# Chunked attention and a squared-ReLU feed-forward on one core: other engines for three squares of the last block, one values step a slot later, and V loads behind transposes in two blocks

## The chip, the cores and the metric

The kernel runs on one core of a Trainium2 chip. The metric is device time in microseconds (us). Five engines with queues of their own matter here: TensorE (PE, with its weight loads listed as PEld), VectorE (DVE), ScalarE (ACT), GpSimd (POOL) and SyncE (SP), which issues nearly all DMAs. Each engine takes its instructions in the order in which the program lists them; an instruction that waits holds back everything behind it on the same engine.

## The reference

For 8 batches and 8 heads, sequences of 576 tokens with 64 values per head are cut into chunks of 64. Attention stays within a chunk. The result, seen as 4608 tokens by 512, goes through a two-layer network with a squared ReLU.

```python
scores = scale * np.matmul(q_c, k_c.transpose(0, 1, 2, 4, 3))     # per chunk of 64
attn = np.exp(scores - max);  attn = attn / (attn.sum(-1) + 1e-09)
out = np.matmul(attn, v_c)
x = out.transpose(0, 2, 1, 3).reshape(B * S, H * D)               # 4608 x 512
h = np.maximum(x @ w_in, 0.0)                                     # 4608 x 2048
return h * h @ w_out                                              # 4608 x 512
```

## The kernel before, in words

The 4608 tokens are 18 groups of 256 tokens (four chunks each); two groups make a block of 512, so there are blocks 0 to 8. Groups 14 and 15 (block 7) collect the ninth chunk of each batch; every other group is "whole", four neighbouring chunks of one batch.

While TensorE runs the feed-forward of block j, the attention of block j+1 (`nxt`) is put between its matmuls, and inputs of block j+2 (`far`) are loaded. The order is written out by hand. A block is a row of **slots**: each `yield` of `ffn_in`/`ffn_in_unit` and then of `ffn_out` ends one. After a slot, one DMA of the list `loads` is issued if the slot's number stands in `go_slots`, and then the steps that `at(slot, step, group)` planned there. For blocks from 3 on, `loads` holds six q and k loads and then nine V loads (first the even heads and odd heads of one group, then of the other; lines 148 and 152). The steps are:

- `C` (`CQ`, `CK`): cast q and k to bf16, on ScalarE for late groups; `TD`: SP's DMA transpose of them (L352);
- `SC`: the 64 score matmuls of a group (L375) and the exponential `e` on ScalarE (L386);
- `AV`: the values product of a group (L403), in two halves t = 0 and 1, each followed on VectorE by a reciprocal `rec` (L410) and a multiplication into `x` (L411);
- `XT`: SP's DMA transpose of `x` into `xT` (L424), which the next block's feed-forward reads.

Scores and values share a pool of two accumulator tiles, `ps_att`. SC of two groups fills both; each half of AV takes one, so half t = 1 of the first group needs the second group's `e` to have been read out, and the halves of the second group's AV need the first group's `x` multiplications done.

Blocks 4 to 8 (`UNITS`) use `ffn_in_unit`. Of the 16 tiles of the hidden layer (`ft`, 128 wide), twelve are done plainly: four matmuls (L608) into an accumulator, a ReLU on ScalarE into a tile `rl` (L572), and a square into `gT`. The square goes to VectorE, GpSimd (both L621, which is the line of the helper `add`) or ScalarE (L575), by a table: `UNIT_SQUARES` for blocks 4 to 7 and `LAST_SQUARES` for block 8, "P" for GpSimd, "A" for ScalarE, VectorE if the tile isn't named. The other four tiles, ft 4 to 7, are computed by seven products instead of eight (L495), one per "u" in `UNIT_ORDER`, in two accumulators `n` and `m` that are held through all seven. I number these steps u1 to u7:

- u1: n, copied to `n1` (ACT, L518). u2: m, and VectorE makes `w = m + n1`.
- u3: n again, copied to `n2` (ACT, L526). u4: m; VectorE makes `c21 = w - m`, GpSimd makes `c12 = w - n2`.
- u5: n; VectorE makes `s = n - n2`. u6: m; VectorE makes `c22 = m + s`, the last reader of m.
- u7: n; ScalarE makes the ReLU of it (L547), GpSimd squares that.

The squared ReLUs of c21, c12 and c22 are three VectorE instructions of another kind, SCALAR_TENSOR_TENSOR (L512), put behind slots 10, 11 and 14. The slots of such a block are: 0 to 2 for ft 8, 9, 10; then u1, ft 11, u2, ft 12, u3, ft 13 (slot 8), u4, ft 14 (slot 10), u5 (11), ft 15 (12), u6 (13), ft 0 (14), u7 (15), ft 1, 2, 3 (16 to 18); then 14 slots of `ffn_out`. The accumulators of the plain tiles come from a pool of four, of which n and m hold two; ft 2's is the one that c22 sets free.

`ffn_out` multiplies the four quarters of `gT` (ft 0 to 7 and 8 to 15, first and second 256 tokens) with the second weight by the same kind of seven products, 16 matmuls each (L661): the first reads ft 8 to 15, the second ft 0 to 7, the others differences that VectorE makes (L621, `w_st<-gT`), beginning with one that needs all of `gT`.

Of the kernel before, what the change touches and what calls it, by code (L numbers as in the profile page):

```python
# [17 lines left out]
def kernel(  # L18
# [31 lines left out]
    def is_whole(g):  # L50
        return chunks[g][0][0] == chunks[g][3][0]
# [104 lines left out]
    def go(pieces):  # L156
        for f in pieces:
            f()
# [279 lines left out]
    SC, AV, XT = scores, values, transpose_x  # L438
# [111 lines left out]

    UNIT_ORDER = (8, 9, 10, "u", 11, "u", 12, "u", 13, "u", 14, "u", 15, "u", 0, "u", 1, 2, 3)
    UNIT_SQUARES = {10: "P", 13: "P", 14: "P", 15: "P", 0: "P", 1: "A", 2: "A", 3: "A"}
    LAST_SQUARES = {10: "P", 13: "P", 14: "P", 12: "A", 1: "A", 2: "A"}
    UNIT_LATER = (10, 11, 14)

    def ffn_in_unit(j):
# [7 lines left out]
        for i, ft in enumerate(UNIT_ORDER):  # L564
            if ft == "u":
                next(products)
            else:
# [4 lines left out]
                nc.scalar.activation(out=rl, in_=h, func=AF.Relu)  # L572
                by = (UNIT_SQUARES if j + 1 < len(blocks) else LAST_SQUARES).get(ft)
                if by == "A":
# [8 lines left out]
    def ffn_in(j, parts, begun={}):  # L583
        if j not in gTs:
            gTs[j] = ffn_pool.tile([128, n_ft, BT], BF16, name="gT")
        gT, xT = gTs[j], xTs[j]
        for u, (c, n, ft) in enumerate((c, n, ft) for c, n, fts in parts for ft in fts):
            h = begun.get(ft)
            if h is None:
                h = ps_ffn.tile([128, 512], FP32, name="ps_ffn")  # L590
            for dt in range(n_dt // 2 if ft in begun else 0, n_dt):
                ffn_in_step(h, xT, c, n, ft, dt)
            if j < 3:
                if n == 512 or u % 2 == 0:
                    rl_tile = ffn_pool.tile([128, 512], FP32, name="rl", bufs=5).bitcast(BF16)
                rl = rl_tile[:, u % 2 * 512:] if n < 512 else rl_tile
            else:
                rl = rl_tile_fp32()
            nc.scalar.activation(out=rl[:, 0:n], in_=h[:, 0:n], func=AF.Relu)  # L599
            if (n == 512 and ft in SQUARES_ON_ACT) or (n < 512 and ft in (12, 3)):  # L600
                nc.scalar.activation(out=gT[:, ft, c:c + n], in_=rl[:, 0:n], func=AF.Square)
            else:
                nc.vector.tensor_tensor(  # L603
                    out=gT[:, ft, c:c + n], in0=rl[:, 0:n], in1=rl[:, 0:n], op=ALU.mult)
            yield
# [17 lines left out]
    def sum_quarters(out, in0, in1, op=ALU.add, half=slice(None)):  # L623
        return lambda _: add(nc.vector, out[:, half], in0[:, half], in1[:, half], op)
# [124 lines left out]
    def ffn_out_by_ft(j):  # L749

        gT = gTs.pop(j)
        n_tt = len(blocks[j]) * GT // 128
        o_ps = [ps_ffn.tile([128, d_model], FP32, name="ps_ffn") for _ in range(n_tt)]

        def mm(tt, ft):
            nc.tensor.matmul(  # L756
                out=o_ps[tt],
                lhsT=gT[:, ft, tt * 128:(tt + 1) * 128],
                rhs=w_out_bf[:, ft, :],
                start=(ft == 0), stop=(ft == n_ft - 1))  # L760


        for ft in range(n_ft - 4):
            for tt in range(n_tt - 1 if ft == 0 else n_tt):
                mm(tt, ft)
                if ft == 1 and tt == n_tt - 2:
                    mm(n_tt - 1, 0)
            yield
        for tt in range(n_tt):
            for ft in range(n_ft - 4, n_ft):  # L770
                mm(tt, ft)
            o_sb = ffn_pool.tile([128, d_model], FP32, name="o_sb", bufs=4)
            nc.scalar.copy(out=o_sb, in_=o_ps[tt])
            b, s0 = chunks[blocks[j][tt // 2]][0]
            t0 = b * S + s0 + tt % 2 * 128
            nc.gpsimd.dma_start(out=out[t0:t0 + 128, :], in_=o_sb)
            yield

    def pieces(grps):
        for g in grps:  # L780
            yield from qk_pieces(g)
        for g in grps:
            yield from v_pieces(g)
# [3 lines left out]
    A, V = nc.scalar.copy, nc.vector.tensor_copy  # L787
# [53 lines left out]
    for j, grps in enumerate(blocks):  # L841
        nxt = blocks[j + 1] if j + 1 < len(blocks) else []
        far = blocks[j + 2] if j + 2 < len(blocks) else []
        plan = {}

        def at(slot, f, g):
            plan.setdefault(slot, []).append((f, g))

        if j == 0:
            loads, go_slots = pieces(far), range(17)  # L850
            at(28, sum_quarters(b11_p_b21, b11, b21), None)
            for slot, f in ((24, TA), (27, SC), (29, AV), (31, XT)):
                at(slot, f, nxt[0])
            at(31, TQ, nxt[1])
            at(31, TK, nxt[1])
            at(31, sum_quarters(b11_m_b22, b11, b22, ALU.subtract), None)
            phases = [first_ffn_in, ffn_out_by_ft(0)]
        elif j == 1:
            loads, go_slots = itertools.chain(*map(qk_pieces, far)), range(26, 48)
            for slot, f in ((4, SC), (8, AV), (12, XT)):  # L860
                at(slot, f, grps[1])
            for i, g in enumerate(nxt):
                for slot, f in ((16 + 4 * i, C), (21 + 4 * i, TD), (36 + i, SC), (38 + 2 * i, AV),
                                (41 + 2 * i, XT)):
                    at(slot, f, g)
            for i, g in enumerate(far):
                at(36 + 4 * i, C, g)
                at(42 + 3 * i, TD, g)
            at(2, sum_quarters(b11_p_b12, b11, b12), None)
            at(12, sum_quarters(b12_p_b22, b12, b22), None)  # L870
            at(20, sum_quarters(b21_p_b22, b21, b22), None)
            phases = [ffn_in(1, [(0, 256, FT_ORDER), (256, 256, FT_ORDER)]), ffn_out(1)]
        else:
            loads, go_slots = pieces(far), range(32)
            slots = {SC: (4, 4), AV: (7, 11), XT: (10, 14), C: (18, 22), TD: (20, 24)}
            if j == 3:
                slots.update({SC: (8, 8), AV: (10, 14), XT: (13, 17)})
                go_slots = [*range(6), *range(13, 32)]
            if not is_whole(nxt[0] if nxt else 0):
                slots.update({SC: (6, 8), AV: (10, 14), XT: (12, 16)})  # L880
            if j == 2:
                loads = itertools.chain(*map(v_pieces, nxt), loads)
                slots = {SC: (8, 10), AV: (12, 15), XT: (15, 18), C: (20, 23), TD: (22, 25)}
                go_slots = [*range(16), *range(25, 36)]
            late_by = 0
            if j in UNITS:
                late_by = 3
                go_slots = [*range(6), *range(13, 17), *range(23, 35)] if j == 4 else range(35)
                slots.update({SC: (4, 4), AV: (8, 13), XT: (12, 17)})
                if not is_whole(nxt[0] if nxt else 0):  # L890
                    slots.update({SC: (8, 8), AV: (10, 14), XT: (14, 18)})
            if j == 3:
                at(2, w_differences, None)
            for f in (SC, AV, XT):
                for i, g in enumerate(nxt):
                    at(slots[f][i], f, g)
            if j > 2 and far and is_whole(far[0]):
                for slot, f, i in ((16, CQ, 0), (18, CK, 0), (18, TD, 0), (18, CQ, 1),
                                   (19, CK, 1), (19, TD, 1)):
                    at(slot + late_by, f, far[i])  # L900
            else:
                for f in (C, TD):
                    for i, g in enumerate(far):
                        at(slots[f][i] + late_by, f, g)
            phases = [ffn_in_unit(j) if j in UNITS else ffn_in(j, [(0, BT, FT_ORDER)]),
                      ffn_out(j)]
        slot = 0
        for phase in phases:
            for _ in phase:
                if slot in go_slots:  # L910
                    for f in loads:
                        f()
                        break
                for f, g in plan.get(slot, []):
                    f(g)
                while late and slot >= LATE_STORES[j]:
                    late.pop(0)()
                slot += 1
        assert all(x < slot for x in plan), (j, slot, sorted(plan))
        go(loads)  # L920
        while late:
            late.pop(0)()
# [30 lines left out]
```

## Time and profile before

| what | us |
|---|---|
| median of the 3 runs (lowest, highest) | 284.1 (282.72, 285.33) |
| the profiled execution's own time | 280.75 |
| its span | 279.0 |
| TensorE busy | 268.4 |
| VectorE, ScalarE, GpSimd busy | 199.2, 156.9, 82.3 |

All times inside a block are taken from the profiled execution, counted from the start of its span. Block 3 runs there from about 110 to 138 us, block 4 to 165, block 5 to 193, block 6 to 221, block 7 to 248 and block 8 to the end. A matmul's recorded end is some time after the next one may begin (they are pipelined), so I read pitches, from start to start: four matmuls of a plain tile 0.86 us, a product of the unit 0.44 us.

### The profile page before, as it was taken

To read this page: it belongs to the slowest core of one execution; us is meant where nothing else is said; L and a number is where in the kernel's file an instruction comes from. 1 tells how busy PE (TensorE), PEld (TensorE's weight loads), DVE (VectorE), ACT (ScalarE), POOL (GpSimd) and SP (SyncE) were. 2 spreads that over 40 slices of the span, in tenths; PEclk is the share of its full clock that TensorE was granted. 3 is DMA by queue.
4 is the path that set the end of the run, shared out by engine and by line. 5 is a ranking of instruction groups with operands and counts; after the bars stand their busy time and mean duration, and the time that the engine had idled before them with its cause. 6 is when DMAs were issued, how large, how long until landed. Compare 5 with 4: busy or idle time off the path is not lost.

```text
span 279.0 us, 7336 instructions
## 1 busy us (share of the span) xinstructions
PE 268.4 (96%) x3020; PEld 182.9 (66%) x3023; DVE 199.2 (71%) x311; ACT 156.9 (56%) x264; POOL 82.3 (29%) x100
## 2 busy tenths in 40 slices
PE   7889999999999999999999999999999999999895
PEld 4543444888774487448765876587558765876484
DVE  0546514998947695579869776987697769876793
ACT  1537605895358853877186927682858276227610
POOL 2037734161169000000029002800470038004412
PEclk9999999999999999999999999999999999999999
DMA  7999999999999999999999999859898942150003
GB/s 236 219 317 361 365 339 237 324 228 191 239 238 194 241 222 203 262 231 195 233 286 239 178 248 253 189 123 221 234 232 180 191 154 53 25 135 18 0 0 150
DMA packets 144384, 57.09 MB, mean 205 GB/s; under 512 B 110624, under 2 KB 141600, under 8 KB 144352
## 3 DMA queue, kind: packets, MB, share of 16 engines
q1 hardware_dynamic: 143296, 53.62, 83.5%
q0 software_dynamic: 912, 2.88, 2.8%
q8 instruction: 23, 0.38, 0.6%
q10 hardware_dynamic: 144, 0.13, 0.1%
q14 instruction: 9, 0.07, 0.1%
HBM read 36.70 MB, written 9.44 MB: 165 GB/s over the span
## 4 chain that ended last, share of the span: by engine, by line
PE 78%; DVE 5%; SPq 4%; DMA 4%; issue 3%; ACT 3%; POOL 2%; POOLq 0%
PE ps_ffn L661 32%; PE ps_ffn L608 32%; PE ps_ffn L756 5%; PE ps_ffn L495 5%; SPq L237 3%; DVE gT L603 2%; DMA qkT<-qkb 2%; PE ps_att L403 2%; DMA w_st<-in_moe_w_in_dram 2%; DVE x L411 1%; PE ps_att L375 1%; ACT rl L599 1%; ACT e L386 1%; POOL gT L621 1%; SPq L228 1%
## 5 line engine op out<-in xcount | busy, mean ns | idle before, releaser
L608 PE MATMUL ps_ffn<-xT,w_in_bf 128*128 128x512 bf16 (+1 forms) x560 | 116.5, 355 | 2.1 <-DVE rl L621 1.4
L608 PEld LDWEIGHTS <-w_in_bf 128*128 128x128 bf16 x560 | 53.5, 98 | 45.0 <-POOL w_in_bf L166 2.0
L621 POOL TENSOR_TENSOR gT<-rl 128x512 bf16<-128x512 f32 x28 | 32.7, 1180 | 131.5 <-ACT rl L572 130.8
L661 PEld LDWEIGHTS <-w_st 128*128 128x128 bf16 x640 | 62.0, 98 | 7.9 <-DVE w_st L621 0.6
L621 DVE TENSOR_TENSOR w_st<-gT 128x2048 bf16<-128x2048 bf16 x40 | 47.4, 1220 | 6.3 <-ACT gT L575 6.2
L603 DVE TENSOR_TENSOR gT<-rl 128x256 bf16<-128x256 bf16 (+2 forms) x67 | 36.0, 573 | 21.6 <-ACT rl L599 20.7
L572 ACT ACTIVATE rl<-ps_ffn 128x512 f32<-128x512 f32 x60 | 35.8, 596 | 22.0 <-PE ps_ffn L608 22.0
L599 ACT ACTIVATE rl<-ps_ffn 128x512 bf16<-128x512 f32 (+2 forms) x80 | 39.0, 511 | 12.4 <-PE ps_ffn L608 11.4
L661 PE MATMUL ps_ffn<-w_out_bf,w_st 128*128 128x256 bf16 x384 | 45.1, 273 | 0.1
L661 PE MATMUL ps_ffn<-w_sum,w_st 128*128 128x256 bf16 x256 | 29.6, 273 | 0.0
L621 DVE TENSOR_TENSOR gT<-rl 128x512 bf16<-128x512 f32 x22 | 15.4, 702 | 17.8 <-ACT rl L572 17.5
L661 PEld LDWEIGHTS <-gT 128*128 128x128 bf16 x256 | 24.6, 98 | 4.9 <-ACT gT L575 0.7
L746 ACT COPY o_sb<-ps_ffn 128x512 f32<-128x512 f32 (+1 forms) x8 | 4.5, 560 | 38.9 <-PE ps_ffn L661 38.9
L411 DVE TENSOR_TENSOR x<-ps_att,rec 128x512 bf16<-128x512 f32 x32 | 22.1, 692 | 1.1
L386 ACT ACTIVATE e<-ps_att 128x1024 bf16<-128x1024 f32 x16 | 15.8, 1022 | 5.1 <-PE ps_att L375 5.1
L512 DVE SCALAR_TENSOR_TENSOR gT<-rl 128x512 bf16<-128x512 f32 x15 | 15.8, 1052 | 0.8 <-POOL rl L621 0.6
L661 PE MATMUL ps_ffn<-w_out_bf,gT 128*128 128x256 bf16 x128 | 15.6, 273 | 0.0
L661 PE MATMUL ps_ffn<-w_sum,gT 128*128 128x256 bf16 x128 | 15.3, 273 | 0.0
L756 PE MATMUL ps_ffn<-w_out_bf,gT 128*128 128x512 bf16 x61 | 14.2, 379 | 0.3 <-issue 0.2
L166 POOL CAST w_in_bf<-w_st 128x1024 bf16<-128x1024 f32 (+1 forms) x9 | 8.6, 959 | 18.8 <-DMA w_st<-in_moe_w_in_dram 18.8
L495 PEld LDWEIGHTS <-w_dif 128*128 128x128 bf16 x100 | 9.3, 98 | 5.3
L341 ACT CAST qkb<-k_sb 128x1024 bf16<-128x1024 f32 x10 | 10.5, 1046 | 1.2 <-DMA k_sb<-in_k_dram 1.2
(81 smaller groups left out, 270.7 us busy)
## 6 DMA issues: line engine op xcount, KB each, us to landing
q_sb<-in_q_dram SPq DMA_DIRECT2D x16, 512.0 KB, 5.8
k_sb<-in_k_dram SPq DMA_DIRECT2D x24, 256.0 KB, 5.9
out_dram<-o_sb SPq DMA_DIRECT2D x20, 256.0 KB, 3.1
w_st<-in_moe_w_in_dram SPq DMA_DIRECT2D x8, 512.0 KB, 7.4
w_st<-in_moe_w_out_dram SPq DMA_DIRECT2D x8, 512.0 KB, 6.1
ve_sb<-in_v_dram SPq DMA_DIRECT2D x28, 128.0 KB, 3.8
vo_sb<-in_v_dram SPq DMA_DIRECT2D x21, 128.0 KB, 3.3
out_dram<-o_sb POOLq DMA_DIRECT2D x9, 256.0 KB, 5.8
```

Source lines behind the costliest of these rows:

```text
L341: copy(out=state["qkb", g][:, 1], in_=qk[g][1].rearrange("p t h d -> p (t h d)"))
L386: nc.scalar.activation(out=e_out, in_=s_in, func=AF.Exp, scale=scale)
L411: nc.vector.tensor_tensor(out=x[:, t].rearrange("p h a d -> p a h d"), in0=o[:, :, :, 0:D], in1=rec.to_broadcast([128, 2, n_hp, D]), op=AL ...
L495: nc.tensor.matmul(out=out[:, 256 * f:256 * f + 256], lhsT=a[:, d, 128 * f:128 * f + 128], rhs=b[:, :, d, :], start=(first and f == 0 and ...
L512: later.append(lambda: nc.vector.scalar_tensor_tensor(out=place_of(i, jj), in0=both(x), scalar=0.0, in1=both(x), op0=ALU.max, op1=ALU.mult))
L572: nc.scalar.activation(out=rl, in_=h, func=AF.Relu)
L599: nc.scalar.activation(out=rl[:, 0:n], in_=h[:, 0:n], func=AF.Relu)
L603: nc.vector.tensor_tensor(out=gT[:, ft, c:c + n], in0=rl[:, 0:n], in1=rl[:, 0:n], op=ALU.mult)
L608: nc.tensor.matmul(out=h[:, 0:n], lhsT=w_in_bf[:, dt, ft * 128:(ft + 1) * 128], rhs=xT[:, c // 128:(c + n) // 128, dt, :], start=(dt == 0) ...
L621: engine.tensor_tensor(out=out, in0=in0, in1=in1, op=op)
L661: nc.tensor.matmul(out=outs[t], lhsT=a[:, i, t * 128:(t + 1) * 128], rhs=b[:, i, :], start=(first and i == 0 and (last or t == 0)), stop=( ...
L756: nc.tensor.matmul(out=o_ps[tt], lhsT=gT[:, ft, tt * 128:(tt + 1) * 128], rhs=w_out_bf[:, ft, :], start=(ft == 0), stop=(ft == n_ft - 1))
```

## The change

Three things change. In block 8, the square of ft 12 goes from ScalarE to VectorE, that of ft 13 from GpSimd to ScalarE, and that of ft 15 from VectorE to GpSimd. In block 6 (the unit block ahead of the groups that are not whole), AV of its two groups moves from slots 10 and 14 to 11 and 15. And `go_slots` leaves gaps: in block 3 slots 18 and 19 carry no load any more, so that five of the nine V loads come behind SP's transposes of x and of q, k; in block 6 the same list that block 4 already had is used, with four V loads in slots 13 to 16 and five from slot 23 on.

```diff
-    LAST_SQUARES = {10: "P", 13: "P", 14: "P", 12: "A", 1: "A", 2: "A"}
+    LAST_SQUARES = {10: "P", 14: "P", 15: "P", 13: "A", 1: "A", 2: "A"}
...
             if j == 3:
                 slots.update({SC: (8, 8), AV: (10, 14), XT: (13, 17)})
-                go_slots = [*range(6), *range(13, 32)]
+                go_slots = [*range(6), *range(13, 17), *range(20, 32)]
...
             if j in UNITS:
                 late_by = 3
-                go_slots = [*range(6), *range(13, 17), *range(23, 35)] if j == 4 else range(35)
+                go_slots = range(35)
+                if far and is_whole(far[0]):
+                    go_slots = [*range(6), *range(13, 17), *range(23, 35)]
                 slots.update({SC: (4, 4), AV: (8, 13), XT: (12, 17)})
                 if not is_whole(nxt[0] if nxt else 0):
-                    slots.update({SC: (8, 8), AV: (10, 14), XT: (14, 18)})
+                    slots.update({SC: (8, 8), AV: (11, 15), XT: (14, 18)})
```

No instruction is added or taken away; on every engine the same kinds and sizes run as before.

## The prediction

> **What bounds the kernel now.** I read the first part of the page, then TensorE's waits, then the stretches of `ffn_in` of three unit blocks, and last the timeline where TensorE stands still. The page:
>
> ```profile
> span 279.0 us, 7336 instructions
> PE 268.4 (96%) x3020; PEld 182.9 (66%) x3023; DVE 199.2 (71%) x311; ACT 156.9 (56%) x264; POOL 82.3 (29%) x100
> ```
>
> TensorE sets the pace: 10.6 us of the span are left, most of them in the start. What an edit can win is what TensorE still waits for in blocks 6 and 8. The stretches (columns after the length: busy us and instructions of PE, PEld, DVE, ACT, POOL, then the granted clock):
>
> ```profile
> 165.40:180.56 15.16, 15.16 (x206) 8.53 (x205) 11.30 (x20) 10.68 (x18) 8.20 (x7) 1.00 0.91 228
> 192.86:208.61 15.75, 15.54 (x207) 8.72 (x205) 11.72 (x20) 10.84 (x18) 8.38 (x7) 1.00 0.97 244
> 248.38:263.32 14.94, 13.57 (x79) 7.46 (x77) 10.08 (x13) 10.06 (x18) 6.10 (x5) 1.00 0.18 43
> ```
>
> Blocks 5, 6 and 8, each at clock 1.00. Block 6 takes 0.59 us more than block 5 for the same work. Block 8 has no attention to do and still takes 14.94, with 1.37 idle. TensorE's waits name both:
>
> ```profile
> PE ps_ffn L608 <- DVE rl L621: 1.4, 1, 1.4
> PE ps_att L403 <- ACT e L386: 0.2, 1, 0.2
> ```
>
> **Block 8.** Its timeline (start, length, engine, line):
>
> ```profile
> 254.24 0.63 ACT L575 ACTIVATE gT<-rl 128x512 bf16<-128x512 f32 x1
> 254.77 0.57 ACT L526 COPY n<-ps_ffn 128x512 f32<-128x512 f32 x1
> 255.92 1.04 POOL L621 TENSOR_TENSOR gT<-rl 128x512 bf16<-128x512 f32 x1 [3.14 <-ACT rl L572]
> 256.92 1.72 POOL L621 TENSOR_TENSOR rl<-nm,n 128x512 f32<-128x512 f32 x1
> ...
> 258.67 1.51 DVE L512 SCALAR_TENSOR_TENSOR gT<-rl 128x512 bf16<-128x512 f32 x1 [0.56 <-POOL rl L621]
> 260.10 0.68 DVE L621 TENSOR_TENSOR gT<-rl 128x512 bf16<-128x512 f32 x1
> 260.70 0.68 DVE L621 TENSOR_TENSOR rl<-ps_ffn,n 128x512 f32<-128x512 f32 x1
> 261.44 1.89 PE L608 MATMUL ps_ffn<-xT,w_in_bf 128*128 128x512 bf16 x8 [1.37 <-DVE rl L621]
> ```
>
> The reader sees a chain: the square of ft 12 on ScalarE holds up the copy n2; GpSimd's c12 waits behind the square of ft 13 and ends at 258.64; VectorE's squared ReLU of c12 waits for it; behind that stand the square of ft 15 and c22, which ends at 261.38; then ft 2 gets its accumulator. ft 1 began at 259.04, so by the pitch of 0.86 ft 2 could have begun at 259.90: the stall is 1.54 us (the 1.37 counts from the modelled end of ft 1).
>
> After the change, with the same durations: n2 follows the ReLU of ft 12 (254.11 to 254.70). c12 stands next behind the square of ft 10, which is long done: 254.75 to 256.05. VectorE: square of ft 12 254.24 to 254.93, c21 255.34 to 256.03, its squared ReLU to 256.75, s to 257.4. The squared ReLU of c12 meets GpSimd's square of ft 14 (256.85 to 257.89). In this trace such an instruction ends 0.55 us after the GpSimd operation that was running (258.67 beside one that ends at 259.63, done at 260.18; the 256.07 one in block 8 likewise), so 258.44. c22 then runs 258.37 to 259.05. That is 0.85 before ft 2 wants its accumulator: the stall goes, 1.54 us. The square of ft 13 on ScalarE (255.53 to 256.16) ends before ft 14's ReLU at 256.20. That of ft 15 on GpSimd ends by 259.5; its reader, the first output product, starts at 261.63.
>
> What is late next: ScalarE's squares of ft 1 and 2 and ReLU of ft 3 run back to back. Before they ended at 264.24, now ReLU of ft 1 260.10, square, ReLU of ft 2, square, ReLU of ft 3, at 0.63 each, end near 263.2; VectorE's square of ft 3 follows, 263.25 to 263.94. The second output product needs it with its fourth matmul, at 261.63 + 1.75 + 0.33 = 263.7. So 0.25 to 0.3 come back as a new wait, and the differences for the third product are as tight. I take **1.25 us gained**; bounds 1.54 and nothing.
>
> A rule speaks against this part. The row: GpSimd's operation at 260.34 took 1.34 instead of 1.04 us beside VectorE's square of 260.10. The Trainium skill, "SBUF — State Buffer", section "Who interferes with whom", says that a VectorE instruction with two inputs in SBUF and a GpSimd one that reads SBUF shut each other out. By it the square of ft 12, new on VectorE, delays c12 by up to 0.2; the sum stays, since c12 isn't needed before 257.4.
>
> **Block 6, values a slot later.** Half t = 1 of the first AV waited for the second `e` until 201.83; whole AV took 0.80 instead of 0.39. One product later it would start at 201.77, t = 1 at 201.94: no wait. Without a new wait, ft 1 of this block would start at 205.25 instead of 205.86, a gain of 0.61. But VectorE's order turns too: s and the squared ReLU of c12 now stand ahead of the first group's `x`. Before:
>
> ```profile
> 201.29 1.59 DVE L512 SCALAR_TENSOR_TENSOR gT<-rl 128x512 bf16<-128x512 f32 x1
> 202.81 0.19 DVE L410 RECIPROCAL rec<-ps_att 128x8 f32<-128x8 f32 x1
> 203.03 0.69 DVE L411 TENSOR_TENSOR x<-ps_att,rec 128x512 bf16<-128x512 f32 x1
> ```
>
> After it: s 202.81 to 203.49; the squared ReLU of c12 is issued at 203.41, while GpSimd squares ft 14 (until 203.78), and ends at 204.33; rec 204.26, x of t = 0 204.48 to 205.17, x of t = 1 205.32 to 206.01. The second AV, at slot 15, would like to start at 204.86, but its halves need those tiles: t = 0 at 205.23, t = 1 at 206.07. ft 1 then starts near 206.33 instead of 205.86. So I count this edit as a **loss of 0.45 us**: 0.6 won, 1.05 paid in a new wait of the second AV for VectorE. Behind it c22 runs 205.93 to 206.6, ahead of ft 2 at 207.2. No trace shows this order; bounds are -0.6 (no wait at all) and +1.5 (GpSimd gets in its next square of 1.04 as well).
>
> **The V loads.** SP issues a V load in 0.5 to 0.6 us. In block 3 two loads stand between the transposes: without them, and with a third gone ahead of the x transpose, the second TD is issued some 1.5 us earlier than at 137.14. It lands 4.1 us after issue, at 141.3, and the second group's scores read it from 142.1: it is not late now. In block 6 the x transposes go ahead of seven and five V loads, and the second TD (issued 218.19, landed 5.5 later at 223.7) is read from 225.1. Block 4 takes 15.16 as block 5 does, and SC in block 7 takes the usual 0.71. So this wins nothing in this trace. What is pushed back are V loads: in block 6 to about 217 to 220, landing near 223, and block 7's AV reads the first group at 228; in block 3 landing near 141, read at 145. Cover of 4 to 5 us; I put **nothing**, with up to 1.2 gained as the bound.
>
> **The sum**: -1.25 + 0.45 + 0 = -0.8 us: 280.75 becomes 279.95. The median of the runs lies 3.35 above the profiled execution; the same 0.8 off 284.1 gives 283.3.
>
> **Rivals.**
> 1. *No new wait in block 6.* For it: the early `x` needs only that the squared ReLU is served before GpSimd's next square; in blocks 4, 5 and 7 the values never wait for VectorE. Against: there five slots lie between the two AVs, here four. -1.25 - 0.6 = -1.85: **282.2**.
> 2. *Transposes are late in runs without a profile.* For: those take 3.35 us more, and the margins above are only 0.8 to 1.4 us. Against: nothing in the trace waits. Then the 1.2 counts: -2.0: **282.1**.
> 3. *Slower: VectorE's queue in block 6 costs more than block 8 gives.* One mechanism: the squared ReLU of c12 is shut out by GpSimd for a second square, `x` comes 1.04 later, and the second AV stands 2.1 us. It decides once that instruction ends after 205.1 instead of 204.33. +1.5 - 1.25 or -1.0: **284.5**.
> 4. *Block 8 doesn't get faster*: TensorE, let go at ft 2, waits as long for the squares of ft 1 to 3. For: ScalarE's last three run without a gap. Against: my count leaves 0.3. About -0.2 + 0.45: **284.3**.
>
> **Chances**: forecast 0.44, rival 1 0.16, rival 2 0.14, rival 3 0.17, rival 4 0.09. The range takes in all of them and about half a microsecond of the runs' own spread: 281.7 to 285.0. One per cent is 2.8 us, about what a measurement of this kernel can tell from no change; no case alone reaches it, rivals 1 and 2 together would with luck. Faster 0.12, same 0.80, slower 0.08.
>
> **What would show it.** In block 8: no wait of L608 for `rl` L621, c12 before 256.3, c22 before 259.9; a short wait of L661 for the square of ft 3. In block 6: no wait of L403 for `e`, but one of 0.4 to 0.6 us twice for `x` L411, and the stretch to the first output product 0.4 to 0.5 longer than 15.75. SP: the second TD of block 3 issued before 136. The prediction is wrong if block 6 gets shorter, if L375 or L403 of blocks 4 or 7 wait for a DMA, or if the first output products stand for more than half a microsecond.

## The result, and the profile after

The changed kernel takes 280.8 us (median of 19 runs, 279.4 to 283.2), the kernel before, run beside it, 283.4 us (19 runs, 281.5 to 285.3). The ratio is 0.9906, with a 95% interval of 0.9883 to 0.9929: 2.7 us faster, 2.0 to 3.3. The forecast was 0.8 us faster, 283.3, with a range that ended at 281.7 below. About 0.7 of the distance between 283.3 and 280.8 is the kernel before itself, whose median was 284.1 in 3 runs and 283.4 in 19; the rest is the effect.

The profiled execution says something else at first sight. First lines of its page:

```profile
span 279.0 us, 7338 instructions
PE 268.0 (96%) x3023; PEld 182.4 (65%) x3023; DVE 198.7 (71%) x311; ACT 156.5 (56%) x264; POOL 81.0 (29%) x100
```

It has the span of the profiled execution of before, 279.0 us, and its own time, 280.80, is the median of its runs. That of before, 280.75, was far below the median of its runs. The profile of the change is already 0.89 us behind when block 3 starts (110.59 against 109.70), ahead of everything that was edited. So the two spans can't be compared as they stand; the stages can. The `ffn_in` stretches of blocks 6 and 8 (columns as before):

```profile
193.57:209.81 16.24, 15.43 (x207) 8.57 (x205) 12.21 (x21) 10.63 (x18) 8.05 (x7) 1.00 0.85 224
249.57:262.99 13.42, 13.42 (x79) 7.44 (x77) 9.88 (x14) 9.53 (x17) 5.59 (x5) 1.00 0.21 50
```

Block 8 has lost its idle time: 13.42 instead of 14.94. Block 6 has got longer: 16.24 instead of 15.75. What happened in block 8 (timeline, as before):

```profile
256.17 1.27 POOL L621 TENSOR_TENSOR rl<-nm,n 128x512 f32<-128x512 f32 x1 [2.04 <-ACT n L526]
...
258.68 1.15 DVE L512 SCALAR_TENSOR_TENSOR gT<-rl 128x512 bf16<-128x512 f32 x1
...
259.75 0.68 DVE L621 TENSOR_TENSOR rl<-ps_ffn,n 128x512 f32<-128x512 f32 x1
...
260.40 2.75 PE L608 MATMUL ps_ffn<-xT,w_in_bf 128*128 128x512 bf16 x12
```

Block 8 starts 1.35 us later here than in the profile before, 0.89 of it from ahead of block 3. c12 begins as soon as n2 is there, c22 ends at 260.43, and ft 1, 2 and 3 run as one piece of twelve matmuls. And block 6 (the squared ReLU of c12, the x multiplication of t = 0, and the two halves of the second AV):

```profile
204.28 0.92 DVE L512 SCALAR_TENSOR_TENSOR gT<-rl 128x512 bf16<-128x512 f32 x1
205.36 0.69 DVE L411 TENSOR_TENSOR x<-ps_att,rec 128x512 bf16<-128x512 f32 x1
```

```profile
206.10 0.22 PE L403 MATMUL ps_att<-ve_sb,e 64*64 64x65 bf16 x2 [0.29 <-DVE x L411]
206.95 0.22 PE L403 MATMUL ps_att<-ve_sb,e 64*64 64x65 bf16 x2 [0.52 <-DVE x L411]
```

The wait for the second `e` is gone, and both halves of the second AV wait for VectorE.

The experiments are read with one table. It gives the time from the first L608 matmul of a block to that of the next one, and for block 8 to the end of the span, in the profiled execution of each kernel.

| kernel | block 4 | block 6 | block 7 | block 8 |
|---|---|---|---|---|
| before | 27.47 | 28.05 | 27.47 | 30.76 |
| before_again | 27.46 | 29.22 | 27.46 | 30.76 |
| before_third | 27.47 | 28.86 | 27.46 | 30.77 |
| the change | 27.47 | 28.54 | 27.46 | 29.45 |
| after_again | 27.46 | 28.53 | 27.46 | 29.48 |
| e1_squares | 27.50 | 29.55 | 27.47 | 29.46 |
| e2_v_block3 | 27.46 | 30.00 | 27.46 | 30.76 |
| e3_v_block6 | 27.48 | 27.87 | 27.47 | 30.77 |
| e4_av_later | 27.70 | 30.14 | 27.47 | 30.76 |
| e5_no_av | 27.47 | 27.87 | 27.54 | 29.47 |
| e7_x_first | 28.12 | 27.86 | 29.13 | 30.77 |
| e8_two_more | 27.54 | 30.71 | 27.46 | 30.67 |
| e9_av_11_16 | 27.47 | 27.67 | 27.47 | 29.47 |
| e10_av_11_16_again | 27.46 | 27.67 | 27.46 | 29.46 |

### The profile page after: what moved, and what is told of

Its sections match the earlier page's. It is cut to its first block, busy times and chain, and to the rows that moved or that the text cites. A ratio compares the mean times of both kernels' runs of the same rounds, so it can differ in the third digit from the quotient of the medians.

```text
span 279.0 us, 7338 instructions
## 1 busy us (share of the span) xinstructions
PE 268.0 (96%) x3023; PEld 182.4 (65%) x3023; DVE 198.7 (71%) x311; ACT 156.5 (56%) x264; POOL 81.0 (29%) x100
## 4 chain that ended last, share of the span: by engine, by line
PE 78%; SPq 8%; DVE 5%; DMA 5%; issue 2%; ACT 1%; POOL 0%
PE ps_ffn L661 32%; PE ps_ffn L608 31%; PE ps_ffn L495 5%; PE ps_ffn L756 5%; SPq L237 3%; DMA w_st<-in_moe_w_in_dram 3%; DMA qkT<-qkb 2%; PE ps_att L403 2%; PE ps_att L375 2%; DVE gT L603 2%; DVE x L411 1%; SPq L148 1%; SPq L152 1%; SPq L352 1%; SPq L228 1%
## 5 line engine op out<-in xcount | busy, mean ns | idle before, releaser
L608 PE MATMUL ps_ffn<-xT,w_in_bf 128*128 128x512 bf16 (+1 forms) x560 | 116.3, 355 | 0.4 <-POOL w_in_bf L166 0.4
L608 PEld LDWEIGHTS <-w_in_bf 128*128 128x128 bf16 x560 | 53.3, 98 | 43.2 <-POOL w_in_bf L166 1.7
L572 ACT ACTIVATE rl<-ps_ffn 128x512 f32<-128x512 f32 x60 | 35.7, 596 | 22.2 <-PE ps_ffn L608 22.2
L661 PEld LDWEIGHTS <-gT 128*128 128x128 bf16 x256 | 24.5, 98 | 5.1 <-ACT gT L575 0.7
L386 ACT ACTIVATE e<-ps_att 128x1024 bf16<-128x1024 f32 x16 | 15.8, 1022 | 5.6 <-PE ps_att L375 5.6
```

What stands on the lines that cost most here:

```text
L386: nc.scalar.activation(out=e_out, in_=s_in, func=AF.Exp, scale=scale)
L608: nc.tensor.matmul(out=h[:, 0:n], lhsT=w_in_bf[:, dt, ft * 128:(ft + 1) * 128], rhs=xT[:, c // 128:(c + n) // 128, dt, :], start=(dt == 0) ...
L661: nc.tensor.matmul(out=outs[t], lhsT=a[:, i, t * 128:(t + 1) * 128], rhs=b[:, i, :], start=(first and i == 0 and (last or t == 0)), stop=( ...
```

## Experiments: one part at a time

Four kernels make one part of the change each, on one chip, beside the kernel before (282.6 us, median of 35 runs).

**Only the squares of block 8.**

```diff
-    LAST_SQUARES = {10: "P", 13: "P", 14: "P", 12: "A", 1: "A", 2: "A"}
+    LAST_SQUARES = {10: "P", 14: "P", 15: "P", 13: "A", 1: "A", 2: "A"}
```

> Only the three squares of block 8 are changed. Theory A (the working of the prediction was right term by term, and what it lacks are the V loads, which save 1.5 to 2 us in executions where transposes land late): 1.3 to 1.6 us faster than before, ratio about 0.995. Theory B (the squares are worth more than the stall at ft 2, since the end of the kernel gains too): 2.5 us faster, ratio about 0.991. In the profile both expect no wait of L608 for c22 (L621).

Measured: ratio 0.9949 (0.9911 to 0.9986), 1.4 us; block 8 takes 29.46 instead of 30.76, 1.30 less. Theory B, that the squares alone make the 2.5 us, falls by the block; the timing alone only just excludes it. The profile showed what I had not seen in that of before. TensorE's waits, SP's queue and TensorE's timeline at the start of block 7:

```profile
PE ps_ffn L608 <- DMA xT<-x: 1.5, 1, 1.5
```

```profile
214.55 1.15 SPq L152 DMA_DIRECT2D vo_sb<-in_v_dram  x2
215.80 2.65 SPq L424 DMA_TRANSPOSE xT<-x  x2
218.54 5.45 SPq L352 DMA_TRANSPOSE qkT<-qkb  x2
```

```profile
222.23 2.75 PE L608 MATMUL ps_ffn<-xT,w_in_bf 128*128 128x512 bf16 x12 [1.52 <-DMA xT<-x]
```

Block 7 can't start: the second transpose of `x`, issued behind nine V loads at 217.18, lands at 222.19. Block 6 takes 29.55 us for it.

**Only block 3's loads.**

```diff
-                go_slots = [*range(6), *range(13, 32)]
+                go_slots = [*range(6), *range(13, 17), *range(20, 32)]
```

> Only the gap in block 3's loads. Theory A: 0.7 to 2 us faster (ratio 0.993 to 0.9975), and in an execution of the kernel before a wait of TensorE at the start of block 4's attention or feed-forward, which is missing here. Theory B: no difference, ratio 1.000 within 0.002.

The gap is slots 17 to 19: the load of slot 17, which stood ahead of the second x transpose, goes as well. Measured: ratio 0.9991 (0.9957 to 1.0024), no difference that this resolves; the gain that theory A wanted here is not to be seen, though up to 1.2 us isn't excluded. Block 6 waits for `xT` here too (1.6 us).

**Only block 6's loads.**

```diff
-                go_slots = [*range(6), *range(13, 17), *range(23, 35)] if j == 4 else range(35)
+                go_slots = [*range(6), *range(13, 17), *range(23, 35)] if j in (4, 6) else range(35)
```

> Only the gaps in block 6's loads. Theory A: between nothing and 1.5 us faster (it is open which of the two blocks carries the gain; with the block-3 loads it makes 1.5 to 2 us). Theory B: no difference, ratio 1.000 within 0.002.

Measured: ratio 0.9949 (0.9913 to 0.9985), 1.4 us. Block 6 takes 27.87, and no matmul waits for `xT`. This is the part that the prediction put at nothing.

**Only the values a slot later.**

```diff
-                    slots.update({SC: (8, 8), AV: (10, 14), XT: (14, 18)})
+                    slots.update({SC: (8, 8), AV: (11, 15), XT: (14, 18)})
```

> Only the values of block 6 a slot later. The prediction's term: 0.45 us slower (ratio about 1.0016) with two waits of L403 for x (L411). Rival: 0.6 us faster (ratio 0.998), no such wait in most executions.

Measured: ratio 1.0020 (0.9985 to 1.0055), which doesn't tell the two apart by itself. The profile does: L403 waits for x (0.7 us, in two waits), and with the wait for `xT` (1.5 us) that this kernel keeps, block 6 takes 30.14.

The four ratios make 2.6 us together, the change made 2.7. Each of the four is known to about a microsecond either way, so an effect of the combination is not needed, but a small one is not excluded.

## Experiments: is it SP's queue?

**The kernel before, profiled again.** Nothing is edited; the question is whether the wait for `xT` belongs to it.

> The kernel before, unchanged, profiled a second time. Theory A (its first profile was an execution in which SP ran ahead of the usual): the second x transpose of block 6 is issued some 24 to 25.5 us after the block's start instead of 22.4, L608 waits 1.5 to 2 us for xT at block 7, and block 6 takes 29.5 to 30.0 us instead of 28.05. Rival (the kernel before has no such wait, and the three experiments that show it brought it in): block 6 at 28.05 again.

> The same a third time: theory A 29.5 to 30.0 us for block 6 with a wait of L608 for xT, the rival 28.05.

Once it shows. SP's queue in the first profile of before, and then in the second, whose block 6 starts only 0.03 us later; then TensorE in the second:

```profile
213.69 2.66 SPq L424 DMA_TRANSPOSE xT<-x  x2
```

```profile
215.19 2.65 SPq L424 DMA_TRANSPOSE xT<-x  x2
```

```profile
221.95 1.24 PE L608 MATMUL ps_ffn<-xT,w_in_bf 128*128 128x512 bf16 x5 [1.19 <-DMA xT<-x]
```

There block 6 takes 29.22. In the third profile it doesn't show: the second transpose lands 25.5 us after the start of block 6, in time, and that block's 28.86 hold another 0.78 ahead of the last matmul of the second AV, which the profile puts down to nothing ("issue"). So the wait is the kernel's own, but not every execution has it: of the six profiles with the old order of loads in block 6 (three of the kernel before, e1, e2, e4), four show 1.2 to 1.6 us of it, two none. All seven with the new order of the change (the change, after_again, e3, e5, e9, e10, and e7 for x) show none.

What sets the four apart can be read from SP's queue. Times in us from the start of block 6; its first q load is the first of its own loads:

| kernel | order of loads | first q load issued | second x transpose issued | landed after | wait of L608 |
|---|---|---|---|---|---|
| before | old | 5.6 | 22.4 | 3.3 | none |
| before_third | old | 5.5 | 22.2 | 3.3 | none |
| before_again | old | 7.6 | 23.8 | 5.3 | 1.2 |
| e1_squares | old | 7.7 | 24.5 | 5.0 | 1.5 |
| e4_av_later | old | 8.0 | 25.3 | 4.8 | 1.5 |
| e2_v_block3 | old | 9.6 | 25.4 | not recorded | 1.6 |
| e3_v_block6 | new | 8.1 | 22.0 | 3.5 | none |
| the change | new | 7.7 | 21.4 | 3.7 | none |

SP is some 2 us or more behind in the four before block 6 has issued a load of its own; from the first q load to the second x transpose all six with the old order take 15.8 to 17.3 us. In the seven profiles with x ahead of the last five V loads SP comes just as late to the q load (7.7 to 9.2), and takes 12.8 to 14.4 us from there. The second part of the wait is the landing: in 3.3 us, the transposes of before_again and e1 would have landed at 27.1 and 27.8, just in time for a block of 27.87, as e3's is. While they were under way the DMA engines nearly stood still, in before_again from 219.8 to 221.7 us and in e1 from 220.4 to 221.9 (5 GB/s, against 207 in the 3.2 us ahead of it). The first profile of before has such a stretch too (220.3 to 221.8), but there the transpose had landed at 218.39. What stops the engines, and what puts SP behind ahead of block 6, wasn't tried.

**Two more DMAs between the x transposes of block 6**, otherwise the kernel before. The data go into a tile that nothing reads.

```diff
+            if j == 6:
+                def extra(t):
+                    b_, s_ = chunks[far[0]][0]
+                    nc.sync.dma_start(
+                        out=v_even[3][0:2 * CH, t, :, 0:D],
+                        in_=v[b_, 0::2, s_ + t * 2 * CH:s_ + (t + 1) * 2 * CH, :].rearrange(
+                            "h s d -> s h d"))
+                at(16, extra, 0)
+                at(16, extra, 1)
```

> The kernel before with two more DMAs of 128 KB between the two x transposes of block 6 (V data into a tile that nothing reads). If SP's issue time ahead of the second x transpose sets the wait: 1.0 to 1.3 us slower than before, ratio about 1.004, with a wait of L608 for xT of 2.5 us or more. If SP's queue isn't what counts: ratio 1.000 within 0.002.

Measured: ratio 1.0033 (0.9998 to 1.0067), and block 6 takes 30.71; the time alone doesn't tell it from the kernel before. The wait has grown by about what the two cost SP to issue. SP's queue and TensorE:

```profile
215.76 1.28 SPq L424 DMA_TRANSPOSE xT<-x  x1
217.09 1.16 SPq L895 DMA_DIRECT2D ve_sb<-in_v_dram  x2
218.35 1.23 SPq L424 DMA_TRANSPOSE xT<-x  x1
```

```profile
222.92 1.45 PE L608 MATMUL ps_ffn<-xT,w_in_bf 128*128 128x512 bf16 x6 [2.47 <-DMA xT<-x]
```

Two issues of 0.58 us each stand between the transposes, and the wait is 2.47 instead of 1.2 to 1.6, in one profile.

**Only x ahead of the loads, not q and k.**

```diff
+                if j == 6:
+                    go_slots = [*range(6), *range(13, 17), *range(19, 24)]
```

> The kernel before; in block 6 the x transposes go ahead of V loads as in the change, but the transposes of q and k stay behind them (V loads in slots 13 to 16 and 19 to 23). Theory X (what costs is that block 7's feed-forward waits for the second x transpose): the wait of L608 for xT is gone and nearly all of the 1.5 us is won, ratio 0.995 to 0.997, unless L375 in block 7 waits for qkT instead. Theory Q (any V load ahead of SP's transposes costs, x or q,k alike): a wait of L375 for qkT of 1 us or more shows in block 7, ratio 0.998 to 1.000.

Measured: ratio 0.9999 (0.9957 to 1.0041); nothing is won. The wait of L608 is gone (block 6 takes 27.86), and block 7 takes 29.13 in its place. SP's queue, with four of the five remaining loads ahead of the second q,k transpose (the first of the four at 216.88), and the scores of block 7:

```profile
217.51 1.09 SPq L148 DMA_DIRECT2D ve_sb<-in_v_dram  x2
218.69 3.33 SPq L352 DMA_TRANSPOSE qkT<-qkb  x1
222.06 0.58 SPq L152 DMA_DIRECT2D vo_sb<-in_v_dram  x1
222.75 2.21 SPq L352 DMA_TRANSPOSE qkT<-qkb  x1
```

```profile
225.25 0.45 PE L375 MATMUL ps_att<-qkT 64*64 64x64 bf16 x32
227.17 0.45 PE L375 MATMUL ps_att<-qkT 64*64 64x64 bf16 x32 [1.48 <-DMA qkT<-qkb]
```

That is theory Q: the last five V loads have to be behind both kinds of transposes. As long as x was late, it hid that q and k were late as well. Compare SP's queue in the changed kernel:

```profile
212.26 1.27 SPq L424 DMA_TRANSPOSE xT<-x  x1
213.57 1.28 SPq L152 DMA_DIRECT2D vo_sb<-in_v_dram  x2
214.95 1.25 SPq L424 DMA_TRANSPOSE xT<-x  x1
216.30 4.06 SPq L352 DMA_TRANSPOSE qkT<-qkb  x2
```

This run's block 4 takes 28.12 us, and there the second group's scores waited 0.47 us for `qkT`: with block 3's loads in the old order its second q,k transpose landed at 142.67, when the scores were due at 142.2. Of the eight profiles with that old order one more shows it, smaller: in e4 (block 4: 27.70) that transpose landed at 143.04, and the second group's weight loads waited 0.18 us for it. Of the six with the new order none does. So block 3's gap is worth a quarter to two thirds of a microsecond in two profiles of eight, too little on average for the timing to show.

## Experiments: the values step

**The change without it** (block 6's AV back to 10 and 14).

> The change without its values step: block 6's AV at slots 10 and 14 as before, the squares and both gaps in the loads kept. If the values step costs 0.5 to 0.65 us, as block 6 showed (28.54 in the changed kernel, 27.87 with block 6's loads alone): about 280 us, ratio 0.988 to 0.990, and block 6 at 27.9 in the profile. If the later values step is worth something with the loads in place: above the changed kernel, ratio 0.993 or more.

Measured: 280.9 us, ratio 0.9910 (0.9873 to 0.9947). By time that is not told apart from the change; by the profile, block 6 takes 27.87 instead of 28.54 (e3's takes 27.87 as well), so the step costs 0.67 us.

**The change, with the second AV another slot later.**

```diff
-                    slots.update({SC: (8, 8), AV: (11, 15), XT: (14, 18)})
+                    slots.update({SC: (8, 8), AV: (11, 16), XT: (14, 18)})
```

> The change, with block 6's second AV at slot 16 instead of 15, one plain tile of 0.86 us later, behind VectorE's x multiplications. If the new wait of AV for x is the whole loss of the values step: block 6 at 27.5 to 27.7 us in the profile (28.54 in the changed kernel), about 0.9 us faster than the changed kernel, ratio 0.987 to 0.988. If VectorE's order costs elsewhere (c22 late for ft 2): block 6 at 28 or more.

Measured: 280.3 us, ratio 0.9910 (0.9870 to 0.9949): the time doesn't show the gain that I expected. Block 6 does, with 27.67; its `ffn_in` stretch has no idle time to speak of:

```profile
194.40:209.77 15.37, 15.35 (x206) 8.54 (x204) 11.38 (x19) 10.69 (x18) 8.04 (x7) 1.00 0.85 220
```

So I ran it once more, beside the changed kernel on the same chip.

> The changed kernel on the same chip as the next one. Ratio 0.990 to 0.992 to before; block 6 at 28.5 us, no wait of L608 for xT.

> The change with block 6's second AV at slot 16, once more, beside the changed kernel. Block 6 at 27.7 us against 28.5; by that 0.85 us faster than the changed kernel, ratio to before lower by 0.003, if nothing else gives it back.

Measured: the change 280.5 us, ratio 0.9893 (0.9865 to 0.9921); this version 279.7 us, ratio 0.9874 (0.9852 to 0.9896). The medians lie 0.85 us apart, as the two block lengths do (28.53 and 27.67). The intervals overlap, so while it is measured that this version beats the kernel before, that it beats the change rests on block 6 of four profiles, two of each.

## Why the prediction was wrong

The forecast was the sum -1.25 + 0.45 + 0. Term by term:

- **Block 8, -1.25**: right. Its block is 1.31 shorter (30.76 to 29.45), the stall of 1.54 that the pitch gave is gone (the stretch lost 1.52). The 0.25 to 0.3 that I let come back before the square of ft 3 are 0.07 in the profile: the fourth matmul of the second output product starts 0.18 after the third instead of 0.11. Some 0.13 came back after the last matmul.
- **Block 6's values, +0.45**: right, 28.54 against 28.05, and for the reason given: x of t = 0 and t = 1 set the two halves free 0.87 and 0.88 after the computed 205.23 and 206.07, in a block that starts 0.87 later. Rival 1, no new wait, falls with that, and so does rival 3: GpSimd didn't get in a second square. The squared ReLU took 0.92, ending 0.55 after the square of ft 14. Against e3 and e5 the loss is 0.67: their block 6 takes 27.87, with the same wait for `e`. The 28.05 of the profile that I worked from hold another 0.18 ahead of the last matmul of the second AV, the place where the third profile loses more; the prediction's 15.75 took that in unseen.
- **The V loads, nothing**: this step failed. They are worth 1.4 us in block 6 (0.4 to 2.5 by timing, 1.2 to 1.6 of TensorE's wait in four profiles). Rival 2, late transposes, was nearest, but I gave it 0.14 and a bound of 1.2, and tied it to runs without a profile and to the transposes of q and k. The one that TensorE waits for is the second transpose of `x`; that those of q and k are late as well shows only when `x` is not (e7).
- **Rival 4** falls: block 8 kept its gain.

How did the step fail? In two ways. The margins that I measured, 0.8 and 1.4 us, are those of the second q,k transpose in blocks 3 and 6. The margin of the second x transpose of block 6 I never worked out: it landed 25.7 us after the block's start, and block 7 needs it at 28.05, so 2.4 us. And I read margins in one execution and took "it is not late now" from it for all of them. In the table above that transpose is issued up to 3.1 us later than in that execution and takes up to 2.0 longer to land; in four profiles of six this made it late.

The total time gave no warning of this. I carried the 3.35 us between the profiled execution and the median along as a constant. They don't come from the way of timing: in every run on record the time exceeds the span by 1.7 to 2.1 us, and the changed kernel's profile lies on its median. But the wait for `xT`, 1.6 us at most in the profiles of that order, isn't all of them either. The third profile of before, 284.49 us, has no such wait; of the 3.7 by which it exceeds the first, 2.9 lie ahead of block 3, and 0.8 in the second AV of block 6. What that stop is wasn't tried.

On the rule weighed for block 8: the Trainium skill, "SBUF — State Buffer", section "Who interferes with whom", would have c12 held up by VectorE's new square where the two meet. c12 took 1.27 us here, as in the blocks without that square beside it; the two overlap by 0.1 us only, so this is no test. Where VectorE's instruction began while GpSimd's ran, the trace agrees with the rule: the squared ReLU of 258.68 took 1.15 instead of the 0.69 of the one at 257.42, and ended 0.55 after GpSimd's square of ft 14.

## What to carry to other kernels

A margin read in one profiled execution is a single sample. Work out the margin of every transfer that an engine waits for, in several profiles, and price a missed one by their spread; the total time of an execution doesn't tell whether its margins are the usual ones (of the three profiles of before, the fastest and the slowest had no wait for `xT`, the middle one had). In a DMA queue that is issued in order, what matters is the place of the few transfers with a due time: put those without one behind all of them, since behind the first late one may stand a second that it hides. And a step moved past a wait on one engine moves past other work on another: here the reordering of VectorE cost more than TensorE's shorter wait had won.

## What was not expected of the hardware

Issuing a DMA on SP is not a fixed cost. In block 6 of the fourteen profiles most V loads took 0.45 to 0.7 us, but the first of them 1.5 to 3.0; a k load took 0.6 to 3.0, and the q,k transposes, all of one size, between 1.6 and 3.5 us. These transposes landed 3.8 to 6.2 us after issue. The last of them landed 30.9 to 33.9 us after the start of block 6 in the six profiles with the old order, and 30.5 to 31.4 in the five with the new one that have a landing recorded.
